# A linear-attention and Fourier feed-forward kernel on one core: new priorities for the planned first part, the plan's order kept for longer, and a last step in tile order

## The chip, the cores and the metric

The kernel runs on one core of one Trainium2 chip. The metric is the device time of the whole kernel in microseconds (us); runs before the change took 1018.55 us in the median of three (1018.1 to 1019.8). The engines are named as the profile names them: PE (TensorE, matrix products), PEld (its weight loads), DVE (VectorE), ACT (ScalarE), POOL (GpSimd) and SP (SyncE, which issues most DMAs).

## The reference

```python
# q, k, v: 8 batches x 8 heads x 576 positions x 64, float32
kv  = einsum('bhsd,bhse->bhde', k, v)
out = einsum('bhsd,bhde->bhse', q, kv)
x   = out / sqrt(mean(out * out, -1) + 1e-6) * g_norm     # then to 8 x 576 x 512
X   = fft(fft(x, axis=1), axis=2)                         # along the sequence, then the channels
u   = x + real(X)
un  = (u - mean(u)) / sqrt(var(u) + 1e-6)                 # over the 512 channels
return u + relu(un @ w_ch1) @ w_ch2                       # 512 -> 2048 -> 512
```

w_ch1 and w_ch2 come as float64 bit patterns and are turned into float32 on the chip.

## The kernel before

The 4608 tokens are nine blocks of 512 tokens. The hidden width of 2048 is cut into 16 slices of 128. A product of the feed-forward part is done three times, as high by high, high by low and low by high part of its two factors, so one block and one slice take 12 matmuls into `ps_h` (L434, first layer) and 12 into four accumulators `acc` (L452, second layer; three matmuls for each of four tiles of 128 tokens). Between them ACT makes the high part `hh` of the result (L444) and DVE the low part `hl` (L447).

There are two parts. The first does, batch by batch: the 64x64 products of k and v (`ps_k`, L618); the turning of q (`ps_q`, L687); the output of the attention (`ps_o`, L713) with its norm (`ss`, `rs_s`, `rs_y`, `ps_y`); the fold of each row with its mirror image (DVE L830 into `ab`, POOL L840 into `xe`, ACT L846 into the high part `xh`, POOL L849 into the low part `xl`); the Fourier sum along the sequence (36 matmuls `ps_f`, L867); the adding and splitting of its halves (ACT L883 `far`, DVE L888 to L897, ACT L905 high part and DVE L908 low part, both into `pt`); the Fourier sum along the channels (36 matmuls `ps_f`, L927); its adding onto `x` (L947, L956, L969, L972); and the turning of `x` into `unT` (`ps_t`, L1028, high part by ACT L1037, low part by DVE L1040). Beside it run the conversion of the weights (raw words, L360 to L379 and L1078; the mean of a column over its rows through a product `ps_w`, L393; L399; L1082, L1087) and the feed-forward products of the first three slices. A batch is called b0 to b7 here, and the 36 matmuls of the sequence sum and of the channel sum "the sequence sum" and "the channel sum" of that batch. The second part does the other 13 slices of all blocks, and writes the result.

The order of the first part comes from a planner (class `Plan`). Each step is an `op` with an engine, a guessed cost in ns, a rank, the steps it comes after and the buffers it takes. `Plan.run` plays the steps on a clock of its own; an engine that falls free takes, of the steps that are ready and get their buffers, the one of lowest rank, and the step's instructions are written at that moment. The rank is 10 for each batch plus the number of the stage, and a table `SHIFT` adds to it for whole groups: a group is a stage, an engine and a rounded rank. While the plan's clock is at or below `PIN_UNTIL` (ns), `Plan.pin` ties each instruction to the one before it on its engine, so that the engine keeps the plan's order. Instructions written later are put in order by the framework's scheduler, which has durations of its own and may move them past each other.

45 steps of two matmuls each (`ps_s`, L507) compute nothing that is used. They have the highest rank, so they stand where the plan finds PE without other work.

The second part is written as a loop: `first` does the first layer of one slice and block, and `second` the second layer of the slice before. In the last call of `second` each accumulator is scaled and added to `uu` by one DVE instruction (L1417) and written out by a DMA of SP (L1420).

Of the kernel before, what the change touches and what calls it, by code (L numbers as in the profile page):

```python
# [14 lines left out]
ALU = mybir.AluOpType  # L15
# [40 lines left out]


SHIFT = {
    ("dft_d", "ACT", -35): -14,
    ("fold", "DVE", 14): -1.5,  # L60
    ("fold", "ACT", 24): 55,
    ("fold", "POOL", 24): 102,
    ("kv", "DMA", 10): 1.5,
    ("out", "ACT", 12): 31,
    ("out", "DVE", 12): -81,
    ("out", "PE", 12): 2,
    ("out", "PE", 22): 87.5,
    ("q", "ACT", 31): -12,
    ("q", "PE", 41): 156.5,
    ("seq", "ACT", 35): -40,  # L70
    ("turn", "DVE", -33): 11,
    ("w", "DVE", 16): -60.5,
    ("y", "DVE", -37): 73.5,
    ("y", "DVE", 13): -35.5,
    ("y", "POOL", 23): -4.5,
}


# [17 lines left out]
class Plan:  # L96
# [34 lines left out]
    def dma(self, kb, rank, emit, after=(), bufs=(), eng="SP"):  # L131
        o = self.op(eng, 600, rank, emit, after, bufs, lag=kb * 4.3)
        o.dma = True
        return o

    def pin(self, emit, now):

        tc = self.tc
        traced = tc.nc.cur_bb.bb.instructions
        start = len(traced)  # L140
        emit()
        traced = tc.nc.cur_bb.bb.instructions
        for i in traced[start:]:
            if i.engine not in self.pinned or now > PIN_UNTIL:
                continue
            last = self.last.get(i.engine)
            if last:
                tc.add_manual_dep(
                    i, last,
                    mybir.DependencyInfo(  # L150
                        mybir.DependencyClass.NoSync, mybir.DependencyReason.DATA
                    ),
                    reason="the plan's order",
                )
# [105 lines left out]
def kernel(  # L260
# [14 lines left out]
    nc = tc.nc  # L275
    B, H, S, D = q.shape
    DM = H * D
    DFF = w2.shape[0]
    P = 128
# [169 lines left out]
    def ffn2(acc, hpair, f, i, first, last):  # L449
        w = w_t[2, f]  # L450
        for n, (a, c) in enumerate(passes):
            nc.tensor.matmul(  # L452
                acc,
                hpair[a][:, i * P : (i + 1) * P],
                w[c],
                start=(first and n == 0),
                stop=(last and n == 2),
            )
# [7 lines left out]
    one = ph1.enter_context(tc.tile_pool(name="one", bufs=1))  # L466
# [47 lines left out]
    dft = {}  # L514
# [647 lines left out]
    for b in range(B):  # L1162
# [32 lines left out]
        for t in range(3):  # L1195
            h, l, z = plan_fold(b, t, xs[t], ys[t], yp, gs[t])
# [158 lines left out]
    def load_u(j):  # L1355
        us[j] = []
        mv = tiny.tile([P, TPB, 2], F32, name="bmv")
        for i in range(TPB):
            n = j * TPB + i
            ut = upool.tile([P, DM], F32, name="uu", tag="uu", bufs=8)  # L1360
            if ascending(n):
                nc.sync.dma_start(ut, u_scr[n * P : (n + 1) * P])
            else:
                nc.gpsimd.indirect_dma_start(  # L1364
                    out=ut,
                    out_offset=None,
                    in_=u_scr[:NTOK],
                    in_offset=bass.IndirectOffsetOnAxis(ap=rowidx[:, n : n + 1], axis=0),
                )
            st = tiny.tile([P, 6], F32, name="bst")  # L1370
            nc.vector.bn_stats(st, ut)  # L1371
            nc.vector.bn_aggr(mv[:, i, :], st)
            us[j].append(ut)
        m = tiny.tile([P, TPB], F32, name="bm")
        nc.vector.tensor_scalar(m, mv[:, :, 1], EPS, None, ALU.add)
        scales[j] = rsqrt_b(tiny, m, rsqrt_a(tiny, m, P, TPB, "b"), P, TPB, "b")
        for i in range(TPB):
            t = j * TPB + i
            part = parts[j][i]
            nc.scalar.activation(  # L1380
                part, part, AF.Identity, scale=scales[j][:, i : i + 1], bias=p0c[:, t : t + 1]
            )
            nc.gpsimd.tensor_tensor(us[j][i], us[j][i], part, ALU.add)  # L1383
# [18 lines left out]
    def second(seg, hpair, f):  # L1402
        j, f0, f1 = seg
        for i in tiles_of[j]:
            if f == f0:
                acc_t[i] = bank("acc")
            ffn2(acc_t[i], hpair, f, i, f == f0, f == f1 - 1)
            if f < f1 - 1:
                continue
            t = j * TPB + i  # L1410
            if f1 < NF:
                part = upool.tile([P, DM], F32, name="up", tag="up", bufs=6)
                nc.scalar.copy(part, acc_t[i])
# [3 lines left out]
            nc.vector.scalar_tensor_tensor(  # L1417
                ut, acc_t[i], scales[j][:, i : i + 1], ut, ALU.mult, ALU.add
            )
            nc.sync.dma_start(out[t * P : (t + 1) * P, :], ut)  # L1420

    prev = None
    step = 0
    for n, seg in enumerate(segs):
        j, f0, f1 = seg
        for f in range(f0, f1):
            if step == 0:
                load_w(*units[0])
                load_w(*units[1])
            if step + 2 < len(units):  # L1430
                load_w(*units[step + 2])
            if f == f0 and n + 1 < len(segs) and segs[n + 1][0] not in held:
# [97 lines left out]
```

## Time and profile before

| what | value |
| --- | --- |
| runs, median (lowest to highest) | 1018.55 us (1018.1 to 1019.8) |
| profiled execution, its own time | 1020.03 us |
| its span, first to last instruction | 1018.2 us |
| mean granted TensorE clock | 0.994 |
| PE busy | 995.1 us (98%), 6070 matmul records |
| DVE, ACT, POOL busy | 497.2, 326.4, 323.6 us (49, 32, 32%) |
| bytes moved by DMA | 140.48 MB, mean 138 GB/s |

The profile is of one execution, whose own time is 1.5 us above the median of the runs; 1.8 us of it lie outside the span. Busy shares are means over two unlike parts: up to about 480 us DVE, ACT and POOL have much to do, after it PE alone. A row of the timeline gives the start, the busy time, engine, line, operation and tiles of one or several instructions, and in square brackets how long the engine had been idle before and which instruction ended that.

### The profile page before, as it was taken

What the parts mean: (1) busy time and instruction counts of PE and PEld (TensorE: products, weight loads), DVE (VectorE), ACT (ScalarE), POOL (GpSimd) and SP (SyncE); (2) the same over time, 40 slices, a digit from 0 to 9 for tenths busy, and PEclk for the clock granted to TensorE, in tenths of its full rate; (3) what the DMA queues carried; (4) which work ended last, traced back from release to release, by engine and by line L of the source; (5) the groups of instructions that cost most, each with busy time, mean ns of one, the idle gap of its engine ahead of it and who ended that gap; (6) DMA issues with size and microseconds to landing.
All of it is one profiled execution on the core that took longest, in us unless ns stands there. A gap on an engine that the chain in (4) does not pass through costs nothing.

```text
span 1018.2 us, 15524 instructions
## 1 busy us (share of the span) xinstructions
PE 995.1 (98%) x6070; PEld 836.4 (82%) x6070; DVE 497.2 (49%) x945; ACT 326.4 (32%) x649; POOL 323.6 (32%) x338
## 2 busy tenths in 40 slices
PE   5999999999999999999999999999999999999997
PEld 4798889889878887888888888888888888888886
DVE  3688976876879779997131313131221311311211
ACT  2565656656534424334221212120120120210110
POOL 1556776875764132226631303020110010200000
PEclk9999999999989999999999999999999999999999
DMA  9888995773425776645552524230310400400101
GB/s 219 210 208 235 267 255 158 228 237 133 163 69 212 269 238 223 222 126 187 166 182 88 162 77 131 86 122 1 150 57 1 166 21 1 165 1 0 42 1 42
DMA packets 109261, 140.48 MB, mean 138 GB/s; under 512 B 51854, under 2 KB 76738, under 8 KB 104580
## 3 DMA queue, kind: packets, MB, share of 16 engines
q1 hardware_dynamic: 105652, 132.02, 41.9%
q0 software_dynamic: 1920, 6.29, 2.1%
q10 hardware_dynamic: 1616, 1.18, 0.4%
q8 instruction: 48, 0.79, 0.3%
q14 instruction: 25, 0.20, 0.1%
HBM read 88.07 MB, written 51.40 MB: 137 GB/s over the span
## 4 chain that ended last, share of the span: by engine, by line
PE 87%; DVE 7%; issue 2%; DMA 1%; POOL 1%; ACT 1%; SPq 0%; DVEq 0%; POOLq 0%; ACTq 0%
PE ps_h L434 36%; PE acc L452 35%; PE ps_f L867 3%; PE ps_o L713 3%; PE ps_k L618 3%; PE ps_f L927 2%; PE ps_s L507 2%; PE ps_q L687 1%; PE ps_t L1028 1%; DVE ab L830 1%; DMA part_scr<-part 1%; DVE wp L379 1%; PE ps_w L393 1%; DVE unTl L1040 1%; DVE ss L740 1%
## 5 line engine op out<-in xcount | busy, mean ns | idle before, releaser
L434 PE MATMUL ps_h<-unTh,w 128*128 128x512 f32 x1152 | 357.6, 392 | 0.1
L452 PE MATMUL acc<-w,hh 128*128 128x512 f32 x1152 | 344.9, 391 | 0.5 <-DVE pm L956 0.5
L447 DVE SCALAR_TENSOR_TENSOR hl<-ps_h,hh 128x512 fp32r<-128x512 f32 x144 | 99.0, 688 | 370.3 <-ACT hh L444 366.2
L434 PEld LDWEIGHTS ps_h<-unTh,w 128*128 128x128 f32 x1152 | 215.5, 188 | 44.7 <-DVE ss L740 0.4
L452 PEld LDWEIGHTS acc<-w,hh 128*128 128x128 f32 x1152 | 214.9, 188 | 44.5 <-PE ps_q L687 0.6
L444 ACT ACTIVATE hh<-ps_h 128x512 fp32r<-128x512 f32 x144 | 85.8, 596 | 461.6 <-PE ps_h L434 442.0
L434 PE MATMUL ps_h<-unTl,w 128*128 128x512 f32 x576 | 224.6, 390 | 0.0
L452 PE MATMUL acc<-w,hl 128*128 128x512 f32 x576 | 213.0, 390 | 0.2 <-DVE hl L447 0.2
L452 PEld LDWEIGHTS acc<-w,hl 128*128 128x128 f32 x576 | 108.0, 188 | 23.3 <-DVE hl L447 0.6
L434 PEld LDWEIGHTS ps_h<-unTl,w 128*128 128x128 f32 x576 | 108.4, 188 | 22.7
L1364 POOL DMA_INDIRECT uu<-u_scr,rowidx x24 | 23.4, 976 | 284.8 <-DVE uu L1417 176.9
L753 POOL TENSOR_TENSOR x<-x,gb 96x512 f32<-96x512 f32 (+1 forms) x42 | 54.5, 1316 | 25.0 <-ACT x L730 23.5
L1383 POOL TENSOR_TENSOR uu<-uu,up 128x512 f32<-128x512 f32 x36 | 45.7, 1297 | 45.7 <-ACT up L1380 45.7
L1417 DVE SCALAR_TENSOR_TENSOR uu<-acc,rs_yb,uu 128x512 f32<-128x512 f32 x36 | 25.2, 745 | 42.5 <-PE acc L452 42.5
L1327 POOL TENSOR_TENSOR w<-wap,w 128x512 fp32r<-128x512 f32 x18 | 23.3, 1294 | 71.3 <-ACT w L1326 71.3
L713 PE MATMUL ps_o<-kvt,fq 64*96 64x64 f32 (+1 forms) x864 | 43.7, 248 | 0.8 <-DVE ss L740 0.8
L713 PEld LDWEIGHTS ps_o<-kvt,fq 64*96 64x96 f32 (+1 forms) x864 | 40.2, 162 | 5.1 <-issue 2.1
L840 POOL TENSOR_TENSOR xe<-ab 96x256 f32<-96x256 f32 (+1 forms) x46 | 36.1, 801 | 21.0 <-DVE ab L830 13.8
L867 PE MATMUL ps_f<-cs,xh 96*128 96x290 f32 (+1 forms) x192 | 41.1, 308 | 0.1
L740 DVE TENSOR_REDUCE ss<-ps_o 96x8 f32<-96x512 f32 (+1 forms) x48 | 31.8, 681 | 18.4 <-ACT ps_o L735 18.4
L830 DVE TENSOR_TENSOR ab<-x 96x254 f32<-96x254 f32 (+5 forms) x69 | 39.2, 622 | 0.1
L1371 DVE BATCH_NORM_STATS2 bst<-uu 128x6 f32<-128x512 f32 x36 | 24.5, 687 | 27.1 <-DMA uu<-u_scr,rowidx 19.1
(125 smaller groups left out, 1047.6 us busy)
## 6 DMA issues: line engine op xcount, KB each, us to landing
raw<-in_moe_w_ch_dram SPq DMA_DIRECT2D x32, 512.0 KB, 7.4
unT_scr<-unTh SPq DMA_DIRECT2D x9, 1024.0 KB, 8.3
unT_scr<-unTl SPq DMA_DIRECT2D x9, 1024.0 KB, 7.4
part_scr<-part SPq DMA_DIRECT2D x36, 256.0 KB, 3.0
unTh<-unT_scr SPq DMA_DIRECT2D x9, 1024.0 KB, 5.1
unTl<-unT_scr SPq DMA_DIRECT2D x9, 1024.0 KB, 7.4
up<-part_scr SPq DMA_DIRECT2D x36, 256.0 KB, 2.8
out_dram<-uu SPq DMA_DIRECT2D x36, 256.0 KB, 2.0
```

The lines of the kernel that those rows point to most:

```text
L434: nc.tensor.matmul(ps, w[c][:, kc * P : (kc + 1) * P], unT[a][:, kc, :], start=(idx == 0), stop=(idx == 3 * KC - 1),)
L444: nc.scalar.activation(hh, ps, AF.Relu)
L447: nc.vector.scalar_tensor_tensor(hl, ps, 0.0, hh.bitcast(F32), ALU.max, ALU.subtract)
L452: nc.tensor.matmul(acc, hpair[a][:, i * P : (i + 1) * P], w[c], start=(first and n == 0), stop=(last and n == 2),)
L618: nc.tensor.matmul(ps.t[s * D : (s + 1) * D, pr * D : (pr + 1) * D], km[:, s, j, :] if j < 4 else kr[:, h, :], vm[:, s, j, :] if j < 4 els ...
L713: nc.tensor.matmul(pss[s].t[:n, at : at + D], fqs[side].t[half, m, :n], kvt.t[half, m], start=True, stop=True,)
L740: nc.vector.tensor_reduce(ss.t[0][:n, :, t, s::2], pss[s].t[:n].rearrange("p (u m e) -> p u m e", u=2, e=D), AX.X, ALU.add,)
L753: nc.gpsimd.tensor_tensor(v_, v_, gb[:n].unsqueeze(1).to_broadcast([n, H, D]), ALU.mult)
L830: nc.vector.tensor_tensor(two_of(ab)[:, :, at : at + width], xx[:, :, lo:hi:step], xx[:, ::-1, DM - lo : DM - hi : -step], ALU.add,)
L840: nc.gpsimd.tensor_tensor(o[:, s], a[:, 0], a[:, 1], ALU.subtract if s else ALU.add)
L867: nc.tensor.matmul(ps.t[:, :NS], xs[t].t[a][:n, part, ch * P : (ch + 1) * P], cs[:n, part, c, t, :], start=(idx == 0), stop=(idx == 8),)
L1383: nc.gpsimd.tensor_tensor(us[j][i], us[j][i], part, ALU.add)
```

## The change

It has four pieces.

- The table `SHIFT` has 36 groups with new numbers instead of 17. A DMA's group is now named by the engine that issues it. All five engines have another order from the first tens of microseconds on.
- `PIN_UNTIL` goes from 260000 to 300000, so more instructions keep the plan's order.
- The matmuls of the last call of `second` are tied to each other in the order in which they are written, which is tile by tile.
- The last tile's last DVE instruction is cut into two halves of 256 columns, and the second half is written out by a DMA of ACT's queue.

```diff
-PIN_UNTIL = 260000
+PIN_UNTIL = 300000
...
 SHIFT = {
-    ("fold", "POOL", 24): 102,
-    ("out", "PE", 22): 87.5,
...
+    ("fold", "POOL", 24): 241,
+    ("out", "PE", 22): 188,
...
+    def in_line(self, engine, emit):
+        start = len(self.tc.nc.cur_bb.bb.instructions)
+        emit()
+        mine = [
+            i for i in self.tc.nc.cur_bb.bb.instructions[start:] if i.engine == engine.engine
+        ]
+        for last, i in zip(mine, mine[1:]):
+            self.tc.add_manual_dep(i, last.name, ...)
...
-            o.rank += SHIFT.get((stage, "DMA" if o.dma else o.eng, round(o.rank)), 0)
+            o.rank += SHIFT.get((stage, o.eng + " DMA" * o.dma, round(o.rank)), 0)
...
-            nc.vector.scalar_tensor_tensor(
-                ut, acc_t[i], scales[j][:, i : i + 1], ut, ALU.mult, ALU.add
-            )
-            nc.sync.dma_start(out[t * P : (t + 1) * P, :], ut)
+            halves = 2 if seg is segs[-1] and i == tiles_of[j][-1] else 1
+            for h in range(halves):
+                cols = slice(h * DM // halves, (h + 1) * DM // halves)
+                nc.vector.scalar_tensor_tensor(
+                    ut[:, cols], acc_t[i][:, cols], scales[j][:, i : i + 1], ut[:, cols],
+                    ALU.mult, ALU.add,
+                )
+                queue = nc.scalar if h else nc.sync
+                queue.dma_start(out[t * P : (t + 1) * P, cols], ut[:, cols])
...
-    second(*prev)
+    plan.in_line(nc.tensor, lambda: second(*prev))
```

The changed file is 35 lines longer above the stages, so L881 there is L846 here, and so on up to the last step. The number of matmuls on PE is the same, the 90 matmuls `ps_s` among them, and the first 17 rows of PE's order are the same. Three places show how rows move; numbers behind a name tell one buffer from another.

The first is ACT's order ahead of the sequence sum of b1. Its rows are the high parts `xh` of the fold, copies out of PSUM (`fq`, `kvt`), the feed-forward's `hh` and two steps of the weight conversion (`w`, `wp`). Before:

```order
L846 ACTIVATE xh_1336<-xe_1232 96x512
L444 ACTIVATE hh_1306<-ps_h_1305 128x512
L1082 ACTIVATE w21_1341<-ps_a_778 128x512
L846 ACTIVATE xh_1345<-xe_1257 96x512
L360 ACTIVATE wp_1350<-raw_775 128x512
```

And after, at the same place:

```order
L881 ACTIVATE xh_1243<-xe_1159 96x512
L726 COPY fq_1194<-ps_q_1193 128x4x96
L881 ACTIVATE xh_1266<-xe_1221 96x512
L726 COPY fq_1204<-ps_q_1203 128x4x96
L664 COPY kvt_1090<-ps_k_1089 128x256
L479 ACTIVATE hh_1251<-ps_h_1250 128x512
L395 ACTIVATE wp_1297<-raw_782 128x512
L1117 ACTIVATE w21_1308<-ps_a_800 128x512
```

The weight step (`w21`, from `ps_a`) that stood between the second and the third `xh` now stands five rows behind the third.

The second is DVE's order between the sequence sum and the channel sum of b6. Its rows are the adding of the halves (`ps_f`), the low parts `pt` that the channel sum reads, the fold `ab` of b7, and small sums. Before, the end of the stretch, from the middle of the fold of the first 96-row tile (`ab_4024`) to the last `pt`:

```order
L830 TENSOR_TENSOR ab_4024<-x_3678 96x2x127
L908 TENSOR_TENSOR pt1_3925<-ps_f_3923,pt0_3924 128x290
L830 TENSOR_TENSOR ab_4024<-x_3678 96x2
L1215 CAST x0h_111<-x0_109 97x24
L890 TENSOR_TENSOR ps_f_3970<-ps_f_3953,far_3999 128x290
L897 TENSOR_TENSOR ps_f_3953<-ps_f_3953,far_3999 128x290
L830 TENSOR_TENSOR ab_4057<-x_3593 96x2x128
L830 TENSOR_TENSOR ab_4057<-x_3593 96x2x127
L830 TENSOR_TENSOR ab_4057<-x_3593 96x2
L1216 TENSOR_TENSOR x0l_112<-x0_109,x0h_111 97x24
L908 TENSOR_TENSOR pt1_3925<-ps_f_3970,pt0_3924 128x290
L908 TENSOR_TENSOR pt1_3925<-ps_f_3953,pt0_3924 128x290
```

After, from the first adding of the halves on:

```order
L923 SCALAR_TENSOR_TENSOR ps_f_3871<-far_3896,paired_107,ps_f_3854 128x290
L930 SCALAR_TENSOR_TENSOR ps_f_3854<-ps_f_3854,paired_107,far_3896 128x290
L943 TENSOR_TENSOR pt1_3856<-ps_f_3871,pt0_3855 128x290
L943 TENSOR_TENSOR pt1_3856<-ps_f_3854,pt0_3855 128x290
L925 TENSOR_TENSOR ps_f_3900<-ps_f_3886,far_3935 128x290
L932 TENSOR_TENSOR ps_f_3886<-ps_f_3886,far_3935 128x290
L943 TENSOR_TENSOR pt1_3856<-ps_f_3900,pt0_3855 128x290
L775 TENSOR_REDUCE ss_3097<-ps_o_3916 97x2x4
L775 TENSOR_REDUCE ss_3097<-ps_o_3917 97x2x4
L943 TENSOR_TENSOR pt1_3856<-ps_f_3886,pt0_3855 128x290
```

The three folds of b7 have left this stretch; two sums `ss` stand in it. On PE the stretch from the sequence sum to the channel sum of b6 holds 18 matmuls `acc` and 12 `ps_h` before, and 16 matmuls `ps_o` and 18 `acc` now.

The third is the end of PE's order, the last step of the second layer with its four accumulators. Before:

```order
L452 MATMUL acc_8896<-w215_5838,hh_9262 128x512 x2
L452 MATMUL acc_8900<-w215_5838,hh_9262 128x512 x2
L452 MATMUL acc_8904<-w215_5838,hh_9262 128x512 x2
L452 MATMUL acc_8908<-w215_5838,hh_9262 128x512 x2
L452 MATMUL acc_8896<-w215_5838,hl_9263 128x512
L452 MATMUL acc_8900<-w215_5838,hl_9263 128x512
L452 MATMUL acc_8904<-w215_5838,hl_9263 128x512
L452 MATMUL acc_8908<-w215_5838,hl_9263 128x512
```

And after:

```order
L487 MATMUL acc_8896<-w215_5838,hh_9262 128x512 x2
L487 MATMUL acc_8896<-w215_5838,hl_9263 128x512
L487 MATMUL acc_8900<-w215_5838,hh_9262 128x512 x2
L487 MATMUL acc_8900<-w215_5838,hl_9263 128x512
L487 MATMUL acc_8904<-w215_5838,hh_9262 128x512 x2
L487 MATMUL acc_8904<-w215_5838,hl_9263 128x512
L487 MATMUL acc_8908<-w215_5838,hh_9262 128x512 x2
L487 MATMUL acc_8908<-w215_5838,hl_9263 128x512
```

The four matmuls on `hl` that stood together at the end now close one tile each.

More of the change, by code (lines that the diff above doesn't have):

```diff
@@ L58 @@
 SHIFT = {
-    ("dft_d", "ACT", -35): -14,
-    ("fold", "DVE", 14): -1.5,
-    ("fold", "ACT", 24): 55,
-    ("fold", "POOL", 24): 102,
[L63 to L66, printed above, removed]
-    ("out", "PE", 22): 87.5,
[L68 to L75, printed above, removed]
+    ("", "SP DMA", -40): -3,
+    ("", "SP DMA", 10): 51.5,
+    ("", "POOL", 40): 15,
+    ("chn", "ACT", 26): 9,
+    ("chn", "ACT", 36): 138.5,
+    ("dft", "ACT", -37): 53,
+    ("dft_d", "SP DMA", -35): 29.5,
+    ("fold", "ACT", -36): 37,
+    ("fold", "POOL", 24): 241,
+    ("fold", "ACT", 44): 56.5,
+    ("kv", "ACT DMA", -40): 142,
+    ("kv", "PE", 30): 104,
+    ("out", "ACT", 2): -42.5,
+    ("out", "PE", 22): 188,
+    ("q", "ACT", -39): 18,
+    ("q", "PE", -39): 15,
+    ("q", "POOL", -39): 58,
+    ("q", "POOL", 11): 54,
+    ("q", "PE", 21): 86,
+    ("q", "ACT", 31): -52,
+    ("q_load", "SP DMA", -39): 31,
+    ("q_load", "SP DMA", 11): -7.5,
+    ("seq", "ACT", 15): -16,
+    ("seq", "PE", 15): 69,
+    ("seq", "ACT", 35): -48.5,
+    ("seq", "PE", 35): -41,
+    ("turn", "DVE", -33): 192,
+    ("turn", "ACT", 27): -61.5,
+    ("turn", "DVE", 37): 10.5,
+    ("w", "DVE", 14): 314.5,
+    ("w", "ACT", 16): -25.5,
+    ("w", "DVE", 16): -62,
+    ("w", "POOL", 16): 92,
+    ("w", "SP DMA", 1005): 1.5,
+    ("y", "ACT", -37): 23.5,
+    ("y", "POOL", 43): -26.5,
 }
@@ L134, in dma @@
         return o
+    def in_line(self, engine, emit):
[5 more added lines that the diff above has]
+        for last, i in zip(mine, mine[1:]):
+            self.tc.add_manual_dep(
+                i, last.name,
+                mybir.DependencyInfo(
+                    mybir.DependencyClass.NoSync, mybir.DependencyReason.DATA
+                ),
+                reason="one tile after another",
+            )
     def pin(self, emit, now):
@@ L1416, in second @@
             ut = us[j][i]
-            nc.vector.scalar_tensor_tensor(
-                ut, acc_t[i], scales[j][:, i : i + 1], ut, ALU.mult, ALU.add
-            )
-            nc.sync.dma_start(out[t * P : (t + 1) * P, :], ut)
+            halves = 2 if seg is segs[-1] and i == tiles_of[j][-1] else 1
[4 more added lines that the diff above has]
+                    ALU.mult, ALU.add,
+                )
+                queue = nc.scalar if h else nc.sync
+                queue.dma_start(out[t * P : (t + 1) * P, cols], ut[:, cols])
     prev = None
```

## The prediction

> **What bounds the kernel now.** I read the page first, then stretches of time, then who makes PE wait, then PE's timeline at those places. The page:
>
> ```profile
> span 1018.2 us, 15524 instructions
> PE 995.1 (98%) x6070; PEld 836.4 (82%) x6070; DVE 497.2 (49%) x945; ACT 326.4 (32%) x649; POOL 323.6 (32%) x338
> ```
>
> PE is idle for only 1018.2 - 995.1 = 23.1 us. A change of order can return idle time and slow clock, nothing else, as the matmuls stay the same. So the table by stretches matters more (start and end; length; busy time of PE, PEld, DVE, ACT, POOL; granted clock; DMA share; GB/s):
>
> ```profile
> 98.80:102.20 3.40, 3.40 (x17) 3.40 (x16) 2.19 (x4) 0.78 (x3) 3.32 (x4) 0.50 1.26 210
> 290.00:296.80 6.80, 6.80 (x29) 5.40 (x29) 3.71 (x11) 1.00 (x3) 5.46 (x6) 0.50 0.06 17
> 300.00:345.00 45.00, 44.28 (x264) 37.88 (x263) 36.04 (x70) 21.43 (x49) 15.05 (x16) 1.00 0.67 241
> 345.00:480.00 135.00, 134.33 (x601) 110.93 (x600) 117.69 (x199) 54.08 (x97) 39.04 (x34) 1.00 0.59 200
> 480.00:1012.00 532.00, 532.00 (x2348) 440.50 (x2348) 116.10 (x222) 84.13 (x139) 77.58 (x66) 1.00 0.24 78
> ```
>
> From 480 to 1012 us PE has no idle time and the full clock: nothing is to be had there. Between the start and 345 us two stretches run at half clock; they cost half their length, 1.7 and 3.4 us. From 300 to 480 us DVE is busy 154 of 180 us, which is little reserve. Who makes PE wait (total, times, longest):
>
> ```profile
> PE ps_w L393 <- DVE wa L1078: 11.8, 1, 11.8
> PE ps_f L927 <- DVE pt L908: 2.0, 1, 2.0
> PE ps_o L713 <- DVE ss L740: 0.8, 2, 0.6
> PE ps_w L393 <- POOL wp L389: 0.7, 2, 0.4
> ```
>
> The 11.8 us are the wait for the first weight; the first 17 rows of PE stay as they are, so I leave them. PE's timeline at the three largest of the others:
>
> ```profile
> 98.41 0.40 PE L867 MATMUL ps_f<-cs,xl 96*128 96x290 f32 x1 [0.82 <-POOL xl L849]
> 286.27 1.58 PE L927 MATMUL ps_f<-cd,pt 128*97 128x130 f32 x16 [0.28 <-ACT pt L905]
> 289.81 2.57 PE L927 MATMUL ps_f<-cd,pt 128*96 128x130 f32 x14 [1.95 <-DVE pt L908]
> ```
>
> The half-clock stretches begin at these two gaps.
>
> **Term A, the sequence sum of b1 (97 to 102 us).** It waits for the third `xl`. Two durations that are needed (the group `ss`, a `xe` alone), and then its chain:
>
> ```profile
> L740 DVE TENSOR_REDUCE ss<-ps_o 96x8 f32<-96x512 f32 (+1 forms) x48 | 31.8, 681 | 18.4 <-ACT ps_o L735 18.4
> 81.84 1.43 POOL L840 TENSOR_TENSOR xe<-ab 97x256 f32<-97x256 f32 x2 [4.94 <-DVE ab L830]
> 89.59 2.66 POOL L840 TENSOR_TENSOR xe<-ab 96x256 f32<-96x256 f32 x2 [0.17 <-DVE ab L830]
> 95.89 0.60 ACT L1082 ACTIVATE w<-ps_a 128x512 fp32r<-128x512 f32 x1 [0.46 <-DVE ps_a L1078]
> 96.38 0.62 ACT L846 ACTIVATE xh<-xe 96x512 fp32r<-96x512 f32 x1
> 97.08 1.27 POOL L849 TENSOR_TENSOR xl<-xe,xh 96x512 fp32r<-96x512 f32 x1 [0.32 <-ACT xh L846]
> ```
>
> `xe` is there at 92.25, but `xh` starts at 96.38, since ACT takes its rows in order and stands at a weight step that waits for DVE. In the new order that step is five rows behind. To compare places I add up each engine's rows in the old and the new order, a matmul at the spacing of its kind, the others at their line's mean in the trace. The sequence sum then stands 4.7 us earlier in PE's work (75.3 instead of 80.0 us): PE asked for the third `xl` at 97.6 (98.41 - 0.82) and will at 92.9. On DVE four sums `ss` of 0.68 us leave the stretch from the channel sum of b0 to the third fold, which ended at 89.4: it ends at 86.7, and with `xe` 1.43, `xh` 0.62, `xl` 1.27 and 0.5 of hand-overs `xl` is there at 90.5. So the wait goes: 0.8 us of idle time and 1.7 of clock, 2.5. What is late next is the weight mean that follows, which hung on the same DVE work before:
>
> ```profile
> 106.84 0.70 DVE wa L1078
> 107.59 1.16 PE ps_w L393 x8
> ```
>
> DVE's work up to it falls by 3.8 us and PE's by 3.3 plus the 2.5 returned, so up to 3.3 + 2.5 - 3.8 = 2.0 us may be given back. I take 0.8: A is 1.7, between 0.5 and 2.5.
>
> **Term B, the channel sum of b6 (286 to 297 us).** Its `pt` come late because DVE does the fold of b7 between them. First a fold alone, and what 16 `ps_o` and 12 `acc` take PE; then the place:
>
> ```profile
> 128.52 0.81 DVE L830 TENSOR_TENSOR ab<-x 96x256 f32<-96x256 f32 x3
> 126.06 1.50 PE ps_o L713 x32
> 876.87 2.72 PE acc L452 x12
> 285.69 3.60 DVE L830 TENSOR_TENSOR ab<-x 96x256 f32<-96x256 f32 x3
> 289.31 0.81 DVE L908 TENSOR_TENSOR pt<-ps_f,pt 128x290 fp32r<-128x290 f32 x2
> 280.84 0.52 DVE L888 SCALAR_TENSOR_TENSOR ps_f<-far,paired,ps_f 128x290 f32<-128x290 f32 x1
> 286.41 2.86 POOL L849 TENSOR_TENSOR xl<-xe,xh 97x512 fp32r<-97x512 f32 x2
> ```
>
> The fold takes 3.60 us beside POOL's work and 0.81 alone. In the new order DVE's rows from the first adding to the last `pt` are four of 0.52, four of 0.41 and two `ss` of 0.68, and no fold: 5.1 us, of which the first half can run before PE ends the sum. PE has 16 `ps_o` (32 records, 1.50 us) and 18 `acc` at 2.72/12 in between, 5.6 us. So the gaps of 0.28 and 1.95 and the clock's 3.4 go: 5.6 us. What is late next is the third fold of b7, which moves behind the turns of b6. ACT's high parts, the turns and the sequence sum:
>
> ```profile
> L1037 ACT ACTIVATE unTh<-ps_t 128x384 fp32r<-128x384 f32 (+14 forms) x80 | 30.1, 499 | 5.2 <-PE ps_t L1028 3.7 <-DVE unTl L1040 1.3
> 328.86 2.15 PE L1028 MATMUL ps_t<-ident,x 97*128 97x97 f32 x24
> 149.16 4.86 PE ps_f L867 x36
> ```
>
> PE's cover from the first turn to the matmul that needs the third `xl` is 24 turns, 27 `acc`, about 0.4 of small ones and six matmuls of the sequence sum: 2.1 + 6.1 + 0.4 + 0.8 = 9.4 us. The chain under it is six high parts on ACT, a low part, the fold, `xe`, `xh`, `xl` and some 0.6 of hand-overs: 6 x 0.5 + 0.5 + 0.81 + 1.43 + 0.62 + 1.27 + 0.6 = 8.2 us at best, and 10.5 with `xe` at 2.66 and the fold at 1.9. So it lies between 1.2 early and 1.1 late, and a late one may cost a half-clock stretch of 1.7 too. I take 0.8 off: B is 4.8, between 2.8 and 5.6.
>
> **Term C, the weight means at 325 and 342 us** (0.7 us by the waits above). DVE's work ahead of the second falls by 3.5 us, but PE comes some 8 us sooner, and DVE has few free microseconds. I take half: 0.35, between -2 and 0.7.
>
> **Term D, the end.**
>
> ```profile
> 1011.80 1.07 PE L452 MATMUL acc<-w,hl 128*128 128x512 f32 x4
> 1012.29 1.41 DVE L1417 SCALAR_TENSOR_TENSOR uu<-acc,rs_yb,uu 128x512 f32<-128x512 f32 x2 [3.51 <-PE acc L452]
> 1014.27 0.74 DVE L1417 SCALAR_TENSOR_TENSOR uu<-acc,rs_yb,uu 128x512 f32<-128x512 f32 x1
> 1015.04 0.33 SPq L1420 DMA_DIRECT2D out_dram<-uu  x1
> DMA to landing us min/median/max: 2.0/2.0/2.0
> L956 DVE SCALAR_TENSOR_TENSOR pm<-ps_f,sgn_t,me 96x258 f32<-96x258 f32 (+1 forms) x48 | 20.9, 476 | 7.4 <-PE ps_f L927 5.0 <-ACT me L947 0.8 <-POOL m L775 0.6
> ```
>
> All four accumulators close within 0.7 us, and DVE then works off four tiles. In tile order three are done while PE still runs. The last matmul ends at 1012.87 as before; `hl` is long there, so the order costs PE nothing. DVE starts at 12.97, two halves of 0.48 (the row of 258 columns; starts 0.40 apart) end at 13.85, and the last DMA leaves at 13.9 instead of 15.04: 1.15 us. It carries half the bytes, so it may land a little sooner. D is 1.3, between 0.5 (ACT's queue slower to issue) and 1.6. By the Trainium skill, "DMA: Bandwidth & Descriptors", "Anatomy of one DMA — SWDGE (gpsimd) path", the larger part of a transfer's time is a fixed 2.0 us and the rest is bytes/436e9, fitted there on the other issuing path; by it the half tile saves an estimated 0.3 us, and D would be 1.45. The trace's 2.0 us for 256 KB lies below that fit.
>
> **Term E, `ps_o` at 34 us** (0.8). It stands behind ten more matmuls now, six fillers and four turns, so part goes: 0.4, between 0 and 0.8. The fillers cost the same in all:
>
> ```profile
> L507 PE MATMUL ps_s<-still 128*128 128x512 f32 x90 | 25.7, 421 | 0.0
> ```
>
> **Term F, waits that no row shows.** Every other hand-over moves too. The sequence sum of b2 (149.16 above) had 1.1 us to spare:
>
> ```profile
> 146.17 1.91 POOL L849 TENSOR_TENSOR xl<-xe,xh 96x512 fp32r<-96x512 f32 x1
> ```
>
> A new gap of b1's kind costs 2.5 us, one of b6's kind 5.6, none 0. I take one small: -2.0. SP's queue has another order too: three loads of k and v of b1 now stand ahead of its two loads of q. PE's turns of that q come after 64 `ps_o` and 12 fillers, which hide them; should they not, that is such a gap.
>
> Sum: 1.7 + 4.8 + 0.35 + 1.3 + 0.4 - 2.0 = 6.55 us. The profiled execution took 1020.03 us (1018.2 and 1.8 around it) and would take 1013.5; its median stands at 1018.55, so I say **1012.0**. All ends at their best give 2.5 + 5.6 + 0.7 + 1.6 + 0.8 = 11.2, or 1007.3.
>
> **Rivals.**
>
> *No new gap and nothing given back.* Then 9 to 11.2 us come back: 1007.3 to 1009.5. For it: the new places lie further from their sources (19 us of PE work between the sequence and channel sum of b1 instead of 9). Against it: DVE at 154 of 180 us.
>
> *One gap of b6's kind remains or is new.* 6.55 + 2.0 - 5.6 = 3 us of gain: 1015.6.
>
> *The half clock is not the gaps' doing.* Then its 5.1 us stay, and a new small gap costs 0.8 rather than 2.5: the gain is 6.55 - 5.1 + 1.7 = 3.1, or 1015.4. Against it: each stretch begins at one of the two longest gaps after the start, and the rows without such a gap have 1.00. The Trainium skill ("TensorE: Matmul & The Clock Gate", "Why this matters for your kernels") warns only of idle gaps above some 3 us, and has the clock fall after an idle window of 3.4 us; by that rule gaps of 0.8 and 2.0 us do not do it. The trace speaks against that rule in the length of the gap and agrees in the step, 3.4 and 6.8 us.
>
> *The waits are only exchanged.* Two gaps of b6's kind, or the new order as good as the old: within 1016.5 to 1020.6.
>
> *Slower: DVE's weight rows before the channel sum of b7.* After the fold the new DVE order has nine weight rows (0.70 us each as `wa` above, 6.3 us) ahead of the adding of b7's halves, and the channel sum is covered by 33 matmuls, 7.5 us. If DVE is 3 us behind, each further microsecond is PE's, with the clock's step on top. It makes the kernel slower from 8.6 us of wait on: 1021 to 1024. Against it: DVE was idle in this stretch before, as 36.04 of 45 us in 300 to 345 show.
>
> **How the numbers follow.** Forecast (1010 to 1014.5): 0.43. No new gap: 0.17. One large gap: 0.17. Clock not the gaps' doing: 0.05. Exchanged: 0.10. Slower: 0.08. The range leaves out the best half of the second case, and the slower case and most of the exchanged one: 1007.5 to 1017.0. About 0.2% (2 us) is what a measurement of this kernel can tell from no change. Faster 0.43 + 0.17 + 0.17 + 0.05 = 0.82; same 0.10; slower 0.08.
>
> **What would show it.** A and B: no idle time of PE at the sequence sum of b1 and the channel sum of b6, and no half clock there. D: the last DVE row ends about 1 us after the last matmul. F: any row of PE with idle time between 60 and 345 us. The forecast is wrong if the new trace has a gap above 1 us at b7's sequence or channel sum, or half clock for more than 3.4 us in all before the end.

## The result: 1009.7 us, and the profile after

The changed kernel takes 1009.71 us in the median of six runs (1008.08 to 1011.38), the kernel before 1018.7 beside it: a ratio of 0.9913, with an interval of 0.9898 to 0.9928. That is 9.0 us less, where 6.55 were forecast, and lies within the range. The profiled execution took 1008.37 us, 1.3 below its median (that of before lay 1.5 above its own), so the two traces differ by more, 1018.2 - 1006.6 = 11.6 us of span. The page's first lines, and the stretches after 280 us (columns as before):

```profile
span 1006.6 us, 15538 instructions
PE 987.5 (98%) x6070; PEld 831.2 (83%) x6070; DVE 488.3 (49%) x946; ACT 326.6 (32%) x649; POOL 322.2 (32%) x338
...
280.00:300.00 20.00, 18.75 (x101) 14.92 (x100) 19.59 (x46) 8.90 (x21) 13.95 (x17) 1.00 0.47 154
300.00:345.00 45.00, 43.94 (x247) 37.53 (x247) 38.31 (x70) 20.20 (x44) 14.49 (x16) 1.00 0.71 249
345.00:480.00 135.00, 135.00 (x607) 112.08 (x606) 110.01 (x187) 54.91 (x96) 48.48 (x41) 1.00 0.59 197
480.00:1002.00 522.00, 522.00 (x2304) 432.24 (x2303) 115.97 (x221) 79.62 (x133) 66.82 (x58) 1.00 0.23 77
```

PE is idle for 1006.6 - 987.5 = 19.1 us instead of 23.1, and busy for 7.6 us less with the same matmuls. Of these 7.6, 5.1 are the clock: in this execution no stretch between the first matmuls (to 17.3 us) and the last one runs at half clock. The other 2.5 lie in the spacing of matmuls that the record counts as busy. Part of that belongs to the waits: a matmul's recorded end lies behind the start of the next one, so the record hides a piece of each gap (in experiment 3 three waits of 1.9 us in all put PE 2.8 us back). PE has four gaps behind the first weight where it had ten; six fewer at 0.3 us each make an estimated 1.8 us. The rest no row shows. Of the 4.0 us of idle time, 1.4 lie behind the last matmul. Who makes PE wait now:

```profile
PE ps_w L428 <- DVE wa L1113: 11.9, 1, 11.9
PE ps_o L1258 <- DVE x0h L1250: 1.2, 1, 1.2
PE ps_w L428 <- POOL wp L424: 1.1, 1, 1.1
PE ps_o L748 <- DVE x L853: 0.6, 1, 0.6
PE ps_o L748 <- ACT fq L726: 0.2, 1, 0.2
```

The sequence sum of b1 and the channel sum of b6 are gone from the list. Their rows, the last operand and PE's first row of the sum, and the two new waits:

```profile
88.46 1.27 POOL L884 TENSOR_TENSOR xl<-xe,xh 96x512 fp32r<-96x512 f32 x1
90.74 0.52 PE L902 MATMUL ps_f<-cs,xh 97*128 97x290 f32 x2
...
274.63 0.46 DVE L943 TENSOR_TENSOR pt<-ps_f,pt 128x290 fp32r<-128x290 f32 x1 [0.17 <-ACT pt L940]
275.53 1.17 PE L962 MATMUL ps_f<-cd,pt 128*97 128x130 f32 x12
...
283.69 1.07 DVE L1250 CAST x0h<-x 97x24 fp32r<-97x24 f32 x1
284.80 0.43 PE L1258 MATMUL ps_o<-cs,x0h 97*8 97x290 f32 x2 [1.23 <-DVE x0h L1250]
...
332.24 0.99 POOL L424 TENSOR_TENSOR wp<-wp,wa 128x128 f32<-128x128 f32 x2
333.28 0.49 PE L428 MATMUL ps_w<-wp,mean_t 128*128 128x128 f32 x2 [1.06 <-POOL wp L424]
```

The third `xl` of b1 ends at 89.73, before the sum starts. The last `pt` of b6 ends 0.4 us before its sum. In exchange PE stands before the nine matmuls on `x0h` (24 columns of `x` that DVE rounds) and before a weight mean. The end, with DVE's last five instructions, the last matmul and the last DMA:

```profile
1000.68 2.87 DVE L1456 SCALAR_TENSOR_TENSOR uu<-acc,rs_yb,uu 128x512 f32<-128x512 f32 x5 [2.15 <-PE acc L487]
1002.23 0.39 PE L487 MATMUL acc<-w,hl 128*128 128x512 f32 x1
1003.63 0.36 ACTq L1461 DMA_DIRECT2D out_dram<-uu  x1
```

PE ends at 1002.62 and DVE at 1003.55; in the kernel before DVE ended 2.1 us after PE (1015.01 - 1012.87).

### The profile page after: what moved, and what is told of

It is laid out like the page before. It is cut to its first block, busy times and chain, and to the rows that moved or that the text cites. A ratio compares the mean times of both kernels' runs of the same rounds, so it can differ in the third digit from the quotient of the medians.

```text
span 1006.6 us, 15538 instructions
## 1 busy us (share of the span) xinstructions
PE 987.5 (98%) x6070; PEld 831.2 (83%) x6070; DVE 488.3 (49%) x946; ACT 326.6 (32%) x649; POOL 322.2 (32%) x338
## 4 chain that ended last, share of the span: by engine, by line
PE 95%; DVE 3%; issue 1%; DMA 0%; POOL 0%; ACT 0%; DVEq 0%; POOLq 0%; ACTq 0%
PE ps_h L469 38%; PE acc L487 38%; PE ps_o L748 4%; PE ps_f L902 4%; PE ps_k L653 2%; PE ps_f L962 2%; PE ps_s L542 2%; PE ps_q L722 2%; PE ps_t L1063 1%; PE ps_w L428 1%; DVE x L853 1%; DMA raw<-in_moe_w_ch_dram 0%; DVE pm L991 0%; DVE ab L865 0%; DVE x L1007 0%
## 5 line engine op out<-in xcount | busy, mean ns | idle before, releaser
L1456 DVE SCALAR_TENSOR_TENSOR uu<-acc,rs_yb,uu 128x512 f32<-128x512 f32 (+1 forms) x37 | 25.4, 730 | 41.1 <-PE acc L487 41.1
L1075 DVE TENSOR_TENSOR unTl<-ps_t,unTh 128x384 fp32r<-128x384 f32 (+14 forms) x80 | 33.0, 472 | 2.8 <-ACT unTh L1072 2.8
```

The lines of the kernel that those rows point to most:

```text
L1075: nc.vector.tensor_tensor(unTs[j].t[1][:, :, to], view()[:, :, lo:hi], unTs[j].t[0][:, :, to].bitcast(F32), ALU.subtract,)
L1456: nc.vector.scalar_tensor_tensor(ut[:, cols], acc_t[i][:, cols], scales[j][:, i : i + 1], ut[:, cols], ALU.mult, ALU.add,)
```

## Experiments

Times are medians beside runs of the kernel before on the same chip (1018.6 to 1019.6 us).

**1. The old last step.** In the changed kernel `halves = 1`, and the last call is plain:

```diff
-            halves = 2 if seg is segs[-1] and i == tiles_of[j][-1] else 1
+            halves = 1
-    plan.in_line(nc.tensor, lambda: second(*prev))
+    second(*prev)
```

> The changed kernel with the old last step (neither the tile order on PE nor the last tile in halves). Theory 1 (the tail is term D, and lies wholly on the path): 1.2 to 1.4 us slower than the changed kernel's 1009.7, so 1011.0, as 1.38 us less lie between the last matmul and the end in the two profiles (5.35 and 3.97). Rival (the end is set by the last DMA, which the halves do not bring forward by as much): 0.5 us, 1010.2. The first part is the same in both; the half clock there may differ from run to run.

Measured: 1011.17 us, ratio 0.9917 (0.9902 to 0.9932). From the end of the last matmul to the end of the span lie 5.36 us, against 3.97 with the new step. Theory 1 gave the right number; the ratio alone could not tell 1.4 from nothing, the trace can.

**2 and 3. Tile order or halves.** Each is taken away by itself, with the lines of experiment 1, in one run each (1010.24 us without the halves, 1012.76 without the tile order). Such single times tell little, as the changed kernel's own runs lie 3.3 us apart; the end of the trace is compared.

> The changed kernel with the last tile's DVE instruction and DMA in one piece; the tile order on PE stays. Read from the last matmul's end to the end of the span (5.35 us with neither, 3.97 with both). Theory 1 (both count: with the tile order three tiles are done when PE ends, one DVE instruction of 0.74 instead of two halves of 0.48 begun 0.40 apart would remain, and 256 KB instead of 128 KB land behind it): 4.3 to 4.6 us. Rival (the tile order does it all): 4.0.

> The changed kernel without the tile order on PE; the last tile stays in halves. Theory 1: DVE still begins its four tiles only when PE has nearly ended, and the halves bring 0.2 to 0.4 us: 5.0 to 5.2 us from the last matmul to the end. Rival (the second DMA queue does it, since SP alone issues four DMAs one behind the other): 4.3 us.

The end without the halves (first two rows), and without the tile order (last three):

```profile
1002.51 2.75 DVE L1456 SCALAR_TENSOR_TENSOR uu<-acc,rs_yb,uu 128x512 f32<-128x512 f32 x4 [2.15 <-PE acc L487]
1004.06 0.39 PE L487 MATMUL acc<-w,hl 128*128 128x512 f32 x1
```

```profile
1004.61 1.07 PE L487 MATMUL acc<-w,hl 128*128 128x512 f32 x4
1005.10 2.85 DVE L1456 SCALAR_TENSOR_TENSOR uu<-acc,rs_yb,uu 128x512 f32<-128x512 f32 x5 [3.50 <-PE acc L487]
1008.03 0.36 ACTq L1461 DMA_DIRECT2D out_dram<-uu  x1
```

Without the halves 4.02 us remain from the last matmul's end (1004.45) to the end of the span (1008.47); without the tile order 5.31 (1005.68 to 1010.99). So the rival of the first holds: the tile order is nearly the whole gain, 1.34 us of it (5.36 - 4.02). The halves by themselves bring 0.05, where theory 1 of the second had 0.2 to 0.4. Two halves end DVE 0.93 us after PE, one piece 0.81 us (1005.26 - 1004.45); the smaller last DMA gets back 0.2 us (2.96 from its issue to the end, instead of 3.18).

**4 to 6. Table and limit apart.** The old table with the new limit, the new table with the old limit, and both old (the kernel before with the new last step alone):

```diff
-PIN_UNTIL = 300000
+PIN_UNTIL = 260000
...
-    (36 groups, with o.eng + " DMA" * o.dma)
+    (17 groups, with "DMA" if o.dma else o.eng)
```

> The changed kernel with the old table of 17 groups (and the old naming of a DMA's group); the plan's order is kept to 300000 and the last step is the new one. Theory 1 (the gain is the table's): the two gaps at the sequence sum of b1 and the channel sum of b6 and their half clock are back, 98 to 102 and 290 to 297 us, and only the tail's 1.4 us remain: 1017.3. Rival (keeping the order for longer cures the channel sum of b6, which lies beyond the old limit): its 5.6 us are gained, 1012 or less.

> The changed kernel with the plan's order kept to 260000 as before. The order is the same up to about 268 us. Theory 1 (the table and the tail make the gain, the limit is worth nothing by itself): within 1 us of 1009.7. Rival A (what the scheduler then does between 268 and 345 us brings a gap of b6's kind): 1.5 to 5.6 us slower, 1011 to 1015. Rival B (the kept order is what makes PE wait 1.2 us for x0h at 283 us): that gap goes, 1008.5.

> The kernel before with nothing but the new last step (tile order on PE and the last tile in halves). Theory 1 (term D, all of it on the path): 3.97 instead of 5.35 us from the last matmul to the end, 1.3 us faster than before. Rival (part of it is hidden behind the last DMA): 0.5 us. With the old table kept to 300000 (1014.3) and the new one kept to 260000 (1015.4) this is the fourth corner of table and limit: if the two simply add, the new table at 260000 and the old one at 300000 together should give what the changed kernel gives (1009.7), that is a corner of 1020.0 here; if this corner lies at 1017.7, the two help each other by 2.3 us.

| table, limit (all with the new last step) | us | ratio to before, interval |
| --- | --- | --- |
| old, 260000 | 1017.64 | 0.9985 (0.9975 to 0.9995) |
| old, 300000 | 1014.33 | 0.9957 (0.9939 to 0.9974) |
| new, 260000 | 1015.40 | 0.9961 (0.9947 to 0.9976) |
| new, 300000 | 1009.56 | 0.9906 (0.9891 to 0.9921) |

The last row is the changed kernel once more, on the chip of the first row:

> The changed kernel once more, as the measure for the next one on the same chip: 1008.1 to 1011.4, median 1009.7.

With both old the new last step alone brings 1.3 us, as theory 1 of the third said. The table alone brings 2.2 us, the limit alone 3.3, both 8.1: some 2.5 us seem to come only together. That figure is not clear of noise: from the four ratios it is 2.7 us, and by their intervals it lies between about 0 and 5.7. The waits show more. The old table with the new limit, two of its waits (first block) and their place:

```profile
PE ps_f L883 <- POOL xl L865: 1.6, 2, 0.8
PE ps_f L883 <- ACT xh L862: 0.9, 1, 0.9
```

```profile
274.49 0.54 PE L883 MATMUL ps_f<-cs,xh 96*128 96x290 f32 x2 [0.89 <-ACT xh L862]
275.84 0.40 PE L883 MATMUL ps_f<-cs,xl 96*128 96x290 f32 x1 [0.82 <-POOL xl L865]
```

The wait of the channel sum of b6 is gone, by the limit alone; two shorter ones stand at the sequence sum of b6 instead, and b1's is as before. In this execution each place is followed by 3.41 us of half clock, from 98.88 and from 276.37 us on. So neither theory holds whole. The new table with the old limit:

```profile
PE ps_o L1258 <- DVE x0h L1250: 6.2, 1, 6.2
```

```profile
284.13 4.93 DVE L865 TENSOR_TENSOR ab<-x 97x256 f32<-97x256 f32 x5
288.98 0.69 DVE L1250 CAST x0h<-x 97x24 fp32r<-97x24 f32 x1
```

Here the framework's scheduler puts b7's fold (4.93 us) ahead of `x0h` on DVE, and PE, which takes its rows in order, stands for 6.2 us; 6.83 us of half clock begin at 287.1. That is rival A, a little beyond its stated end (1015.4 against 1015). With the new table the limit is worth that much because it keeps `x0h` ahead of the fold.

**7. The price of a gap.** Both new waits are longer than b1's old one, and no half clock follows. So I put twelve gaps into the second part, each before a first layer:

```diff
+        for n, cols in enumerate(STALL.get(step, ())):      # 64 to 5 x 512 columns
+            if n == 0:
+                nc.tensor.matmul(ps, w_t[1, f][0][:, :P], unTs[j][0][:, 0, :], start=True, stop=True)
+            nc.scalar.activation(hh[:, :cols], ps[:, :cols], AF.Relu)
         ffn1(ps, w_t[1, f], unTs[j])
...
```

Here and in experiment 8 PE keeps the written order from the first of these places on (these lines are left out above), and there is one run of each.

> The changed kernel with twelve gaps put into the part of PE that has none (about 700 to 960 us, 22 us apart): before a first layer PE does one matmul more, ACT copies its result one to five times (64 to 512 columns each), and the first layer's matmuls wait for that. Estimated idle times of PE: 0.4, 0.75, 1.05, 1.15, 1.35, 1.65, 1.75, 1.95, 2.25, 2.35, 2.55, 3.1 us. Theory 1 (as predicted: a gap of 0.8 us and more is followed by half clock): eleven half-clock stretches of 3.41 us. Theory 2 (the clock follows the work that PE does in each stretch of a fixed 3.413 us raster; in the trace of before the stretches that were followed by half clock hold 57% and 35% of PE's time as work, in the trace of after 60% and 66% are not followed by it): none for gaps below 1.4 us, for those between 1.4 and 2.8 us it depends on how the raster cuts them, and always above 2.8 us, so three to six stretches, starting on one raster. Theory 3 (only gaps above 3 us count): one or none.

The gaps were 0.31, 0.69, 3.71 (ACT had other work), 1.10, 1.32, 1.63, 1.73, 1.95, 2.25, 2.36, 2.58 and 3.21 us. Four of the last, and the clock (the column after POOL's) around them:

```profile
860.54 0.73 PE L469 MATMUL ps_h<-unTh,w 128*128 128x512 f32 x2 [1.95 <-ACT hh L1437]
885.08 0.73 PE L469 MATMUL ps_h<-unTh,w 128*128 128x512 f32 x2 [2.25 <-ACT hh L1437]
911.37 0.73 PE L469 MATMUL ps_h<-unTh,w 128*128 128x512 f32 x2 [2.36 <-ACT hh L1437]
936.23 0.73 PE L469 MATMUL ps_h<-unTh,w 128*128 128x512 f32 x2 [2.58 <-ACT hh L1437]
```

```profile
742.80:886.20 143.40, 133.42 (x582) 108.50 (x581) 25.86 (x45) 26.47 (x46) 6.96 (x6) 1.00 0.16 58
886.20:889.60 3.40, 3.40 (x10) 2.62 (x9) 1.75 (x4) 0.00 (x0) 1.50 (x2) 0.50 0.53 164
889.60:937.40 47.80, 42.86 (x188) 34.83 (x187) 7.92 (x17) 12.38 (x21) 5.45 (x5) 1.00 0.04 11
937.40:940.80 3.40, 3.40 (x10) 2.62 (x9) 0.00 (x0) 0.00 (x0) 0.00 (x0) 0.50 0.00 0
```

Four gaps lost the clock, each for one stretch of 3.41 us, at 739.44, 886.21, 937.41 and 964.72: after 3.71, 2.25, 2.58 and 3.21 us. Those starts are 43, 15 and 8 times 3.413 us apart, so they lie on one fixed raster. The gap of 2.36 us, longer than that of 2.25, cost nothing more: the raster's line at 910.11 cut it into 1.10 and 1.26. The largest idle time within one stretch that kept the clock is 1.63 us, the smallest that lost it 2.02. Theory 2 holds, and theory 1 falls for matmuls on 128 rows; so does theory 3, as gaps of 2.25 and 2.58 us lost the clock. The Trainium skill ("TensorE: Matmul & The Clock Gate", "Part 1: The HAM clock gate") has a window of 3413 ns that runs freely; the starts agree. The rule of the Trainium skill in the same page's "Why this matters for your kernels", that gaps above some 3 us matter, is not borne out: 2.25 us lost the clock.

**8. Rows in use.** b1's gap had only 0.90 us of idle time in its stretch, so something else counts too. Matmuls of 512 columns without any wait, at eight places:

```diff
+        k, m, n = STALL.get(step, (0, 0, 0))      # rows, columns of weights, 32 times
+        for _ in range(n):
+            nc.tensor.matmul(ps[:m], w_t[1, f][0][:k, :m], unTs[j][0][:k, 0, :], start=True, stop=True)
...
```

> The changed kernel with 32 more matmuls of 512 columns (7.2 us, so at least one whole stretch of the 3.413 us raster) at eight places of the second part, without any wait: on 32, 64 and 96 rows with 128 columns of weights, on 128 rows with 32, 64 and 96 columns of weights, 64 rows with 64, and 128 with 128. Their result is overwritten. Theory 1 (the clock follows the time in which PE works): no half clock anywhere. Theory 2 (it follows the work weighted by the rows in use, since the stretch of 57% that lost the clock was of 96 rows, so 43%, and in the gap series 53% at 128 rows kept it and 40% lost it): half clock behind the stretches on 32 rows (25%), and perhaps on 64 (50%), none on 96 rows or for fewer columns. Theory 3 (weighted by the cells in use): half clock also for 32 columns (25%) and for 64 by 64 (25%).

```profile
691.32 11.70 PE L1436 MATMUL ps_h<-unTh,w 32*128 32x512 f32 x32
732.62 7.57 PE L1436 MATMUL ps_h<-unTh,w 64*128 64x512 f32 x32
...
694.10:707.70 13.60, 13.60 (x33) 10.03 (x32) 0.00 (x0) 0.00 (x0) 0.00 (x0) 0.50 0.00 0
732.60:740.20 7.60, 7.60 (x34) 5.91 (x33) 0.00 (x0) 0.00 (x0) 0.00 (x0) 1.00 0.49 208
```

On 32 rows PE loses the clock though it never stands still, and for four stretches; on 64 and 96 rows, and with 32, 64 or 96 columns of weights, it keeps it. So theory 2 again, for a stream of one kind: rows count, columns of weights do not. The matmuls of the first part are on 64 rows (`ps_o`), 96 or 97 (`ps_f` of the sequence sum), so a short gap among them may weigh more than one in the feed-forward part. That is not shown. If the time of each matmul, up to the start of the next, is counted by its share of 128 rows, the stretches of the raster in the trace of before do not fall in order: the one from 33.94 us holds 46% and keeps the clock, b1's from 95.38 us holds 54% and loses it.

It is still a matter of luck whether such a gap loses the clock. In the kernel before with the new last step, whose first part is the same as before, b1's gap is the same and the clock stays, though that stretch holds 0.95 us of idle time instead of 0.90. A gap of 0.97 us at another wait then brings 6.8 us of half clock:

```profile
98.69 0.40 PE L883 MATMUL ps_f<-cs,xl 96*128 96x290 f32 x1 [0.82 <-POOL xl L865]
104.86 0.90 PE L729 MATMUL ps_o<-kvt,fq 64*96 64x64 f32 x16 [0.97 <-ACT fq L707]
...
99.30:102.70 3.40, 3.40 (x28) 3.40 (x27) 2.34 (x4) 0.55 (x2) 3.23 (x5) 1.00 1.22 220
106.10:112.90 6.80, 6.80 (x60) 6.22 (x60) 5.95 (x11) 4.06 (x9) 4.83 (x6) 0.50 1.22 272
```

The trace of before has no wait at that place: the half clock had already made PE 1.2 us later there (its `ps_o` start at 104.23 instead of 102.99), and `fq` was ready.

The nine runs of the old table with the new limit show the same: four at a clock of 1.000 took 1012.4 to 1013.0 us, two at 0.997 and 0.998 took 1014.3 and 1014.6, three at 0.994 and 0.995 took 1017.2 to 1018.5. One program, 6 us apart, some 5 of them by the clock (a mean of 0.995 is about 10 us at half clock, which cost half their length). The runs of before had 0.993 to 0.998, those of the changed kernel 0.999 to 1.000.

**9. Moving the two waiting steps.** The nine matmuls on `x0h`, and the weight mean with the subtraction after it, are held back until six matmuls of the following first layer are written:

```diff
+        if emit.__name__ in HELD and (self.held or not self.gone(emit)):
+            self.held.append(emit)
+            return
...
         for kc in range(KC):
+            while kc == 2 and plan.held:
+                plan.held.pop(0)()
...
```

> The changed kernel with two steps of PE put behind the first six matmuls of the first layer that follows them: the nine matmuls on x0h at 283 us and the weight mean at 332 us. Nothing else moves by more than a few rows. Theory 1 (PE's two longest gaps, 1.23 and 1.06 us, are due to the place of these two steps in its order; they cost their own length and no clock): both gaps go, 2.3 us faster than the changed kernel, 1007.4. Theory 2 (the gaps are the visible end of a DVE that is behind; the wait only moves to the next step that needs it): 0 to 1 us faster, with new waits for DVE at 286 to 345 us. Theory 3 (these gaps also bring half clock in a part of the runs, by where the raster cuts them): 2.3 us and up to 1.7 more in the median, 1006, and a narrower spread of the runs.

Measured: 1008.77 us, ratio 0.9889 (0.9874 to 0.9904), beside 0.9906 for the changed kernel: the intervals overlap. Both waits are gone; a new one stands in the place of the first:

```profile
292.30 1.05 PE L1073 MATMUL ps_t<-ident,x 96*128 96x96 f32 x8 [0.72 <-DVE wa L1123]
```

PE comes to the next step that needs DVE 1.2 us sooner, and DVE, busy 19.59 of 20 us there in the changed kernel, is no faster. Theory 2 holds for `x0h`: 1.2 us are gained there and lost again by 300 us.

**10 and 11. The order kept for longer, and the mean alone moved.**

```diff
-PIN_UNTIL = 300000
+PIN_UNTIL = 345000
```

> The changed kernel with the plan's order kept to 345000. Rows move on PE, DVE and ACT between about 297 and 345 us only. Theory 1 (a kept order gives what the table was searched for): the wait of 1.1 us at 332 us goes, 1008.5. Rival (there the scheduler's order is no worse, since DVE is the one that is behind): within 1 us of 1009.7, with a wait at another weight mean. In either case no half clock before the end in most runs.

Measured: 1008.20 us, ratio 0.9891 (0.9874 to 0.9907). The wait of the mean stays, 1.0 us, so theory 1 falls in what it named; the time lies 1.4 us below the changed kernel's in experiments 4 to 6, by intervals that overlap. With the mean held back as in 9, but not `x0h`:

> The changed kernel with the plan's order kept to 345000, and with the weight mean at 331 us and the subtraction that reads it put behind the first six matmuls of the first layer that follows. Theory 1 (this wait, 1.0 us for POOL's sum, is only a matter of place, since DVE's next use of the mean had 2 us to spare): it goes and nothing takes its place, 1.0 us faster than the order kept to 345000 alone (1008.2, ratio 0.9891), so 1007.2 and a ratio of 0.988. Theory 2 (as with the step on x0h, which gave 1.2 us and had 0.9 and 0.5 taken back by the next steps that wait for DVE at 291 to 293 us): 0 to 0.4 us.

```profile
PE ps_o L1274 <- DVE x0h L1266: 1.2, 1, 1.2
PE ps_o L758 <- DVE x L863: 0.5, 1, 0.5
PE ps_o L758 <- ACT fq L736: 0.2, 1, 0.2
```

Measured: 1006.27 us, ratio 0.9884 (0.9867 to 0.9901). The wait of the mean is gone and nothing stands in its place, as theory 1 said. In the trace PE gains 1.3 us on experiment 10 at that place. The medians do not tell it from noise: the ratio of experiment 10 was 0.9891, 0.7 us more, with an interval that covers nearly all of this one. This is the lowest time of all; its interval and that of the changed kernel (0.9891 to 0.9921 in experiments 4 to 6) still overlap a little.

**What the spread of the changed kernel is made of.** Its runs lie 3.3 us apart, with hardly any half clock behind the first matmuls. In six of the traces of kernels with its first part (experiments 1, 2, 3, 7, 8 and 9) PE waits for 0.7 to 1.9 us between 373 and 389 us, and falls 1.3 to 2.8 us back by it; in the others it falls back by 0.4 at most. In experiment 3, and in the changed kernel at the same place:

```profile
374.60 0.59 ACT L1179 COPY part<-acc 128x512 f32<-128x512 f32 x1 [6.72 <-DMA part_scr<-part]
376.40 1.43 PE L487 MATMUL acc<-w,hh 128*128 128x512 f32 x5 [1.05 <-ACT hh L479]
```

```profile
371.14 0.59 ACT L1179 COPY part<-acc 128x512 f32<-128x512 f32 x1 [3.57 <-DMA part_scr<-part]
```

ACT waits 6.7 instead of 3.6 us until a write of 256 KB has freed its buffer, and `hh` stands behind that copy on ACT. Why that write is later in some executions no run here tells.

Another part lies at the start. The first matmuls run at half clock, and this ends sooner in some executions. The same 16 matmuls in the changed kernel and in experiment 11:

```profile
15.61 1.12 PE L653 MATMUL ps_k<-vm,km 128*64 128x64 f32 x16
```

```profile
15.33 0.69 PE L663 MATMUL ps_k<-vm,km 128*64 128x64 f32 x16
```

Behind it PE is 1.0 us earlier in experiment 11 (its next such group starts at 17.79 instead of 18.77) and 0.9 us earlier in experiment 10. Over all traces with these first rows it lies up to 1.3 us apart (17.77 in experiment 8, 19.10 in experiment 3). So 1.0 of the 2.3 us by which the span of experiment 11 (1004.3) is shorter than the changed kernel's (1006.6) is luck at the start, and 1.3 are the mean.

## Why the prediction was right, point by point

The time lies in the range, but the likeliest case (1010 to 1014.5) was 0.3 us too slow, and 9.0 us of gain stand against 6.55. Between the two traces the gain is 11.6 us, 5.0 more than the sum; one was of a good execution and the other of a poor one. Against its terms, in the traces:

- **A** (1.7, by 2.5 - 0.8): both parts of the 2.5 came back, 0.8 us of idle time and 1.7 of clock, and nothing was given back at the weight mean at 101 us. The third `xl` came at 89.7, forecast was 90.5. So the 0.8 taken off were not lost. But experiment 6 shows that the 1.7 of clock are lost there only in some executions, and that in the old order PE then waits 0.97 us for `fq` instead, a wait that this argument did not have.
- **B** (4.8, by 5.6 - 0.8): the 5.6 came back. What was to be late next, the third fold of b7, was not; `x0h`, which that argument did not have, was, by 1.23 us. The prediction argued from the new order as a whole and did not ask what the limit does in it. Experiment 4 shows that the limit alone removes this wait, and experiment 5 that the table without the limit puts 6.2 us of another in its place.
- **C** (0.35): the two means cost 0.7 us before, one of them 1.06 now: -0.4, within the stated ends. Experiment 11 shows that this was a matter of place.
- **D** (1.3): 5.35 - 3.97 = 1.38. Right in size, wrong in one part: the cutting in halves was counted at 0.48 + 0.40 against 0.74, and gains nothing (experiment 2).
- **E** (0.4): the wait at 34 us is gone, 0.8.
- **F** (-2.0): the size is right by luck, and the step behind it failed. New gaps did come, by the waits above 0.6, 1.2 and 0.2 us, 2.0 in all, and with the mean's 1.06 two are longer than b1's. But the term stood for one small gap priced as "b1's kind, 2.5", a gap with its half clock, while here three came and none had a half clock behind it. At the prediction's own price, 1.7 more for each gap above 0.8 us, the two would have cost 3.4 us more. The mechanism was right, half clock behind gaps, and its condition was wrong: not the length of the gap, but how much idle time falls into one stretch of a fixed raster (experiment 7), with the rows in use beside it (experiment 8, for unbroken streams).
- **What no term had.** The prediction said that a change of order can return "idle time and slow clock, nothing else"; PE's busy time fell by 2.5 us beyond the clock. And three waits of before, 0.48 us at 181 us and 0.17 and 0.50 at 394 to 396, stood in no term and are gone, 1.2 us; the last two are luck, as waits of that kind are back at 384 to 389 us in six other traces. These 3.7 us, the 1.6 that A and B took off in vain and E's 0.4, less C's 0.75, make up the 5.0.

The rival that the half clock is not the gaps' doing is refuted by experiment 7, for gaps of 2 us and more within a stretch; "no new gap" came nearest in time (1007.3 to 1009.5) but for another reason, since new gaps did come. Of the two signs named for a wrong forecast, a gap above 1 us at b7's sums and half clock for more than 3.4 us, neither came.

## What to carry to other kernels

Price a gap of the matmul engine in two parts: its length, with the piece that the record hides (some 0.3 us here), and the half clock behind it, which depends on where it lies on the raster and, by what the streams show, may depend on how many rows the matmuls around it use. A table of priorities and the point up to which its order is kept are one thing: the new table kept only to the old limit brought a wait of 6.2 us. Each alone gave 2 to 3 us here, together 8. For the last step, let each accumulator close as early as it can, so that the work behind it runs beside the matmuls; cutting the last piece in two brought next to nothing. And a profile is one execution: here two executions of the same order could differ by 1 us at the start and by 1 to 3 us at one place later on.

## What the runs showed of the hardware

- The clock falls for whole stretches of one raster of 3.413 us. On 128 rows 1.63 us of idle time within a stretch kept it, 2.02 lost it; gaps of 1.95 and 2.36 us kept it when the raster cut them.
- A stream on 32 rows without any gap brought 13.6 us of half clock; 64 rows kept it, and so did 32 columns of weights on 128 rows.
- The half clock of the first matmuls ended at different points of the program, which put PE up to 1.3 us apart.
- Where exactly the bound lies for mixed matmuls stays open: b1's gap of 0.82 us lost the clock in one execution and kept it in another, and counting the matmuls by their rows does not put the stretches in order.
